# A decode layer on one core: weight rows in blocks of four, a bias added later, and stream buffers on 4 KB boundaries

## The chip, the cores and the metric

The kernel runs on one core of a Trainium2 chip. The metric is device time in microseconds (us) of one execution. Most executions of one kernel agree within 0.3%, which is 2 us here. Each kernel of the experiments was timed in rounds beside the kernel before, on the same chip.

## The reference

One decode step of a transformer layer in bf16: attention over a long cache, then an MLP with the mish activation.

```python
# B=4 sequences, one token each, D=640, H=32 heads, Sk=4096 cached keys, Dh=128, F=1728
q = (layernorm(x) @ wq)                              # wq [640, 4096]
p = softmax(q @ k_cache^T * Dh**-0.5)                # k_cache, v_cache [4, 32, 4096, 128]
h = x + (p @ v_cache) @ wo                           # wo [4096, 640]
g = layernorm(h) @ w1 + b1                           # w1 [640, 1728], b1 [1728]
act = g * tanh(log1p(exp(-|g|)) + max(g, 0))         # mish
out = h + act @ w2                                   # w2 [1728, 640]
```

The two caches are 268 MB of the 283 MB that the kernel reads.

## The kernel before

In what follows PE is the matmul engine, DVE the vector engine and ACT the activation engine; SP only issues loads and stores. A load has "landed" on a DMA engine when that engine has reported its share of it as done.

Everything large goes through four stream slots of 32 KB a partition. A cache tile is 4 MB: 128 partitions of one 32768 B row each. There are 64 such loads (the last is cut into four), and the weights travel in the same queue: wq first, wo between the tiles and at the end, then w1 into a slot, then w2 into a buffer of its own.

The sizes that matter: `P` = 128; `FM` = 13 full blocks of 128 MLP columns; `FT` = 64 columns left over, the "tail"; `DC` = 5 blocks of 128 in D; `FC` = 14; `N` = 4.

```python
consts = ctx.enter_context(tc.tile_pool(name="consts", bufs=1))
stream = ctx.enter_context(tc.tile_pool(name="stream", bufs=NSLOT))   # 4 slots, behind consts
...
w2_sb = consts.tile([P, FM, D], BF16)
W1S = (0, 2, 4, DC)
W2S = (0, 5, 10, FM)

def load_mlp():
    w1_slot = stream.tile([P, SLOT], BF16, tag="s", name="w1_slot")
    ...
    for c0, c1 in zip(W1S, W1S[1:]):                    # w1: three loads of 2, 2, 1 row blocks
        nc.sync.dma_start(out=w1_sb[:, c0:c1, :], in_=w1_v[:, c0:c1, :])
    w2_v = B_w2[0 : FM * P, :].rearrange("(p j) n -> p j n", j=FM)   # 13 rows per partition
    for j0, j1 in zip(W2S, W2S[1:]):                    # w2: three loads, 5, 5, 3 rows a partition
        nc.sync.dma_start(out=w2_sb[:, j0:j1, :], in_=w2_v[:, j0:j1, :])
...
# at the start: b1 turned onto partitions by the load itself, 26 B (and 2 B) a partition
nc.scalar.dma_start(out=b1T[:, 0:FM], in_=B_b1[0 : FM * P].rearrange("(p j) -> p j", j=FM))
nc.scalar.dma_start(out=b1T[0:FT, FM : FM + 1], in_=B_b1[FM * P : F].rearrange("(p o) -> p o", o=1))
...
        if i == 0:                                      # after the first cache tile
            nc.scalar.dma_start(out=w2_tail[0:FT, :], in_=B_w2[FM * P : F, :])
            nc.scalar.dma_start(out=w2_tail[FT : FT + CG, :], in_=B_w2[F - CG : F, :])
...
# MLP, at the end. b1 goes into the sum over w1, so it is multiplied by std first
b1s = b1T * std                                         # (cut to its meaning)
for c0, c1 in zip(W1S, W1S[1:]):
    if c1 == DC:
        nc.tensor.matmul(h1_ps[:, :, :], lhsT=ident_f[:, :], rhs=b1s[:, :, :], start=False, stop=False)
    for j in [FM] + list(range(FM)):
        for c in range(c0, c1):
            if j < FM:                                  # every 13th column of w1
                w = w1_sb[:, c, 0 : FM * P].rearrange("p (f j) -> p j f", j=FM)[:, j, :]
            else:
                w = w1_sb[:, c, FM * P : F]
            nc.tensor.matmul(h1_ps[0 : (P if j < FM else FT), j, :], lhsT=w, rhs=cen[:, c, :], ...)
h1 = h1_ps * rstd                                       # (cut to its meaning)
# ... mish: one activation and five vector operations, giving act
for j in [FM] + list(range(FM)):                        # 56 output matmuls
    for k in range(CG):
        nc.tensor.matmul(y2_ps[...], lhsT=act[0:rows, j, :],
                         rhs=w2_sb[:, j, cs] if j < FM else w2_tail[0:FT, cs], ...)
nc.vector.tensor_copy(out=o_bf[:, :], in_=y2_ps[:, :])  # then the store
```

A partition holds 13 consecutive rows of w2 so that each load has long rows. The price is that block `j` of the hidden vector is every 13th column of w1.

The softmax here doesn't subtract the row's maximum and nothing guards it: scores larger than these inputs give would overflow.

## Time and profile before

| | before |
|---|---|
| time, median of the first 3 runs | 669.73 us (669.3 to 670.16) |
| time, median of 6 runs, at the comparison | 669.35 us (668.91 to 670.16) |
| span of the profiled execution | 667.5 us |
| busy: PE, DVE | 426.0 us (64%), 411.7 us (62%) |
| bytes moved by DMA, mean rate | 283.81 MB, 425 GB/s |
| 32768 B packets (8192), median, mean | 1213, 1217.0 ns |
| 5120 B, 3456 B, 1280 B packets, median | 196, 135, 55 ns |

These lines are from the page of the kernel before. The span is cut into 40 slices. "DMA" is the mean busy share of the 16 DMA engines in tenths (9 means 90% or more), the next line the rate in each slice. The q lines give packets, megabytes and share of the engines' time: q1 is the SP queue with the stream, q10 the ACT queue with the small loads, and q8 instruction fetches.

```profile
DMA  9999999999999999999999999999999999999995
GB/s 376 440 411 438 419 438 435 432 427 439 432 427 430 430 436 429 438 437 423 432 437 431 433 428 436 437 430 427 434 437 436 429 429 432 438 431 430 427 415 241
DMA packets 12591, 283.81 MB, mean 425 GB/s; under 512 B 1608, under 2 KB 1680, under 8 KB 3728
q1 hardware_dynamic: 12224, 283.27, 98.8%
q8 instruction: 23, 0.38, 0.2%
q10 hardware_dynamic: 336, 0.10, 0.1%
```

The DMA engines are full in every slice but the last. The stream sets the time up to about 650 us. Only the last 15 us or so offer another choice. This is the end of the chain of waits that finished last (start, duration, what):

```profile
641.55 15.31 DMA w_slot<-in_B_w_dram
656.86 0.04 issue
656.90 1.89 PE h_ps L537 x28
658.80 0.52 PE h_ps L528 x2
659.32 1.02 PE h_ps L537 x14
...
661.91 0.23 DVE act L576
662.14 0.04 issue
662.18 2.16 PE y_ps L585 x55
664.34 0.02 issue
664.37 0.33 DVE o_bf L591
```

The second w1 load has landed at 656.86. Its 28 matmuls, the b1 matmul, the 14 matmuls of the third load, mish and the output matmuls follow without a gap. The last w2 load does not appear. Its landing is in the trace all the same: 658.38 us on the DMA engine that finished first, 662.96 on the one that finished last. A load is there only when the slowest of 16 engines is done.

Two groups of the timeline (start, duration, engine, line, operation, count) show why the choice of columns costs time:

```profile
649.25 0.67 PE L409 MATMUL y_ps<-a_2706,wo_late 128*128 128x4 bf16 x20
654.79 1.91 PE L537 MATMUL h_ps<-cen,w_slot 128*64 128x4 bf16 x28
```

Matmuls of one output size take 33 ns with wo's contiguous columns (0.67 us over 20) and 68 ns with every 13th column of w1 (1.91 over 28).

### The profile page before, as it was taken

To read this page: it belongs to the slowest core of one execution; us is meant where nothing else is said; L and a number is where in the kernel's file an instruction comes from. 1 tells how busy PE (TensorE), PEld (TensorE's weight loads), DVE (VectorE), ACT (ScalarE), POOL (GpSimd) and SP (SyncE) were. 2 spreads that over 40 slices of the span, in tenths; PEclk is the share of its full clock that TensorE was granted. 3 is DMA by queue.
4 is the path that set the end of the run, shared out by engine and by line. 5 is a ranking of instruction groups with operands and counts; after the bars stand their busy time and mean duration, and the time that the engine had idled before them with its cause. 6 is when DMAs were issued, how large, how long until landed. Compare 5 with 4: busy or idle time off the path is not lost.

```text
span 667.5 us, 6967 instructions
## 1 busy us (share of the span) xinstructions
PE 426.0 (64%) x2937; PEld 198.2 (30%) x2937; DVE 411.7 (62%) x477; ACT 75.5 (11%) x312; POOL 1.9 (0%) x9
## 2 busy tenths in 40 slices
PE   1967546694567675574764865568765657747586
PEld 0323222242223332232332422233322223323145
DVE  3387565686565676465675666557765657757542
ACT  0401001010001110011100110101100111001011
POOL 1000000000000000000000000000000000000000
PEclk9987789897788976788877788979867898778895
DMA  9999999999999999999999999999999999999995
GB/s 376 440 411 438 419 438 435 432 427 439 432 427 430 430 436 429 438 437 423 432 437 431 433 428 436 437 430 427 434 437 436 429 429 432 438 431 430 427 415 241
DMA packets 12591, 283.81 MB, mean 425 GB/s; under 512 B 1608, under 2 KB 1680, under 8 KB 3728
## 3 DMA queue, kind: packets, MB, share of 16 engines
q1 hardware_dynamic: 12224, 283.27, 98.8%
q8 instruction: 23, 0.38, 0.2%
q10 hardware_dynamic: 336, 0.10, 0.1%
q14 instruction: 8, 0.07, 0.0%
HBM read 283.36 MB, written 0.01 MB: 424 GB/s over the span
## 4 chain that ended last, share of the span: by engine, by line
DMA 61%; DVE 19%; PE 18%; issue 1%; ACT 0%; SPq 0%; DVEq 0%; ACTq 0%
DVE prod L284 16%; PE red L296 14%; DMA k_1005<-in_A_k_cache_dram 4%; DMA k_530<-in_A_k_cache_dram 4%; DMA k_1480<-in_A_k_cache_dram 4%; DMA k_1955<-in_A_k_cache_dram 4%; DMA k_2881<-in_A_k_cache_dram 4%; DMA k_2428<-in_A_k_cache_dram 4%; DMA k_3334<-in_A_k_cache_dram 4%; DMA k_1691<-in_A_k_cache_dram 4%; DMA k_310<-in_A_k_cache_dram 4%; DMA k_3092<-in_A_k_cache_dram 4%; DMA k_1216<-in_A_k_cache_dram 3%; DMA k_741<-in_A_k_cache_dram 3%; DMA v_3666<-in_A_v_cache_dram 3%; DMA k_2166<-in_A_k_cache_dram 3%
## 5 line engine op out<-in xcount | busy, mean ns | idle before, releaser
L296 PE MATMUL red<-prod,ident 128*128 128x512 bf16 x1024 | 300.1, 451 | 218.9 <-DVE prod L284 218.0
L296 PEld LDWEIGHTS <-ident 128*128 128x128 bf16 x1024 | 116.0, 114 | 385.2 <-issue 317.6
L313 DVE TENSOR_REDUCE s_f<-red 128x32 f32<-128x512 f32 x128 | 88.1, 688 | 79.4 <-PE red L296 79.2
L316 ACT ACTIVATE ex<-s_f 128x32 bf16<-128x32 f32 x128 | 29.3, 229 | 516.6 <-DVE s_f L313 516.6
L323 DVE TENSOR_TENSOR e<-ex,hmask 128x128 bf16<-128x128 bf16 x128 | 36.5, 285 | 6.1 <-ACT ex L316 6.1
L373 PEld LDWEIGHTS o_ps<-selo,pv_sb 128*128 128x128 f32 x256 | 34.0, 194 | 6.0 <-ACT pv_sb L363 1.2
L352 PEld LDWEIGHTS <-e 128*16 128x16 bf16 x1024 | 22.6, 89 | 36.8 <-issue 15.5
L373 PE MATMUL o_ps<-selo,pv_sb 128*128 128x4 f32 x256 | 31.1, 245 | 0.7 <-ACT pv_sb L363 0.7
L316 ACT ACTIVATION_READ_ACCUMULATOR ex<-s_f 128x1 f32 x128 | 23.9, 187 | 0.1
L284 DVE TENSOR_TENSOR prod<-k_79,qbc 128x4096 bf16<-128x4096 bf16 x4 | 9.1, 2287 | 17.6 <-DMA k_79<-in_A_k_cache_dram 17.6
L379 DVE TENSOR_TENSOR OT<-o_ps,rl 128x16 bf16<-128x16 f32 x8 | 1.6, 195 | 21.0 <-PE o_ps L373 21.0
L256 PE MATMUL q_ps<-wq_74,lnT 128*4 128x512 bf16 x32 | 10.7, 470 | 4.7 <-DMA wq_74<-in_A_wq_dram 4.7
L284 DVE TENSOR_TENSOR prod<-k_1691,qbc 128x4096 bf16<-128x4096 bf16 x4 | 9.1, 2286 | 5.7 <-DMA k_1691<-in_A_k_cache_dram 5.7
L284 DVE TENSOR_TENSOR prod<-k_3092,qbc 128x4096 bf16<-128x4096 bf16 x4 | 9.1, 2286 | 5.7 <-DMA k_3092<-in_A_k_cache_dram 5.7
L284 DVE TENSOR_TENSOR prod<-k_1216,qbc 128x4096 bf16<-128x4096 bf16 x4 | 9.1, 2286 | 4.9 <-DMA k_1216<-in_A_k_cache_dram 4.9
L284 DVE TENSOR_TENSOR prod<-k_3545,qbc 128x4096 bf16<-128x4096 bf16 x4 | 9.1, 2286 | 4.9 <-DMA k_3545<-in_A_k_cache_dram 4.9
L284 DVE TENSOR_TENSOR prod<-k_741,qbc 128x4096 bf16<-128x4096 bf16 x4 | 9.1, 2285 | 4.9 <-DMA k_741<-in_A_k_cache_dram 4.9
L284 DVE TENSOR_TENSOR prod<-k_903,qbc 128x4096 bf16<-128x4096 bf16 x4 | 9.1, 2287 | 4.8 <-DMA k_903<-in_A_k_cache_dram 4.8
L284 DVE TENSOR_TENSOR prod<-k_428,qbc 128x4096 bf16<-128x4096 bf16 x4 | 9.1, 2286 | 4.6 <-DMA k_428<-in_A_k_cache_dram 4.6
L284 DVE TENSOR_TENSOR prod<-k_1378,qbc 128x4096 bf16<-128x4096 bf16 x4 | 9.1, 2286 | 4.5 <-DMA k_1378<-in_A_k_cache_dram 4.5
L284 DVE TENSOR_TENSOR prod<-k_1853,qbc 128x4096 bf16<-128x4096 bf16 x4 | 9.1, 2286 | 4.5 <-DMA k_1853<-in_A_k_cache_dram 4.5
L284 DVE TENSOR_TENSOR prod<-k_530,qbc 128x4096 bf16<-128x4096 bf16 x4 | 9.1, 2285 | 4.4 <-DMA k_530<-in_A_k_cache_dram 4.4
(179 smaller groups left out, 376.2 us busy)
## 6 DMA issues: line engine op xcount, KB each, us to landing
wq_74<-in_A_wq_dram SPq DMA_DIRECT2D x1, 4096.0 KB
k_79<-in_A_k_cache_dram SPq DMA_DIRECT2D x1, 4096.0 KB, 24.8
k_81<-in_A_k_cache_dram SPq DMA_DIRECT2D x1, 4096.0 KB, 33.9
v_83<-in_A_v_cache_dram SPq DMA_DIRECT2D x1, 4096.0 KB, 17.3
k_244<-in_A_k_cache_dram SPq DMA_DIRECT2D x1, 4096.0 KB
v_246<-in_A_v_cache_dram SPq DMA_DIRECT2D x1, 4096.0 KB
k_310<-in_A_k_cache_dram SPq DMA_DIRECT2D x1, 4096.0 KB, 24.6
v_314<-in_A_v_cache_dram SPq DMA_DIRECT2D x1, 4096.0 KB, 32.1
```

The lines of the kernel that those rows point to most:

```text
L256: nc.tensor.matmul(q_ps[:, :], lhsT=lnT[:, c, :], rhs=wq_t[c // WQC][:, o : o + 512], start=(c == 0), stop=(c == DC - 1),)
L284: nc.vector.tensor_tensor(out=t[:, :, :], in0=kt[i][:, s * RS : (s + 1) * RS, :], in1=q_bc[hg][:, b, :].unsqueeze(1).to_broadcast([P, RS, ...
L296: nc.tensor.matmul(red[:, :, :], lhsT=ident[:, :], rhs=t[:, :, c * CW : (c + 1) * CW], start=(c == 0), stop=(c == Dh // CW - 1),)
L313: nc.vector.tensor_reduce(out=s_t[i][:, sl], in_=reds.pop((i, s))[:, :, :], axis=AX.X, op=ALU.add)
L316: nc.scalar.activation(out=ex_t[i][:, sl], in_=s_t[i][:, sl], func=ACT.Exp, scale=SCALE, accum_out=rs_t[hg][:, b, s : s + 1],)
L323: nc.vector.tensor_tensor(out=e_t[i][:, sl, :], in0=ex_t[i][:, sl].unsqueeze(2).to_broadcast([P, RS, G]), in1=hmask[:, :].unsqueeze(1).to_ ...
L352: nc.tensor.matmul(pvs[i % 2][k * QD : k * QD + RQ * G, :], lhsT=e_t[i][:, u * RQ : (u + 1) * RQ, :], rhs=vt[i][:, u * RQ : (u + 1) * RQ, ...
L373: nc.tensor.matmul(o_ps[hg][:, b, :], lhsT=t[:, r, :], rhs=selo[:, r, :], start=(r == 0), stop=(r == RQ - 1),)
L379: nc.vector.tensor_tensor(out=OT[:, hg * G : (hg + 1) * G, :].rearrange("p g b -> p b g"), in0=o_ps.pop(hg)[:, :, :], in1=rl.pop(hg)[:, :] ...
```

## The change

It has three intents. The slots shall start on 4 KB boundaries: 20480 B into the partition instead of 57600 B, which is 256 B past one. The MLP's rows are taken in blocks of four per partition, so that w1 is read at every 4th column instead of every 13th. And b1 is added behind rstd by one vector addition, so that its scaling and its matmul go. The loads change with it: w2 comes in four loads (three of 4 rows, one of 1 row a partition), its 64-row tail moves from the ACT queue near the start to the SP queue right before them, and b1 moves from the start to behind tile 1 and is cut into smaller pieces.

```diff
+    front = ctx.enter_context(tc.tile_pool(name="front", bufs=1))
+    stream = ctx.enter_context(tc.tile_pool(name="stream", bufs=NSLOT))
     consts = ctx.enter_context(tc.tile_pool(name="consts", bufs=1))
-    stream = ctx.enter_context(tc.tile_pool(name="stream", bufs=NSLOT))
...
-    W2S = (0, 5, 10, FM)
+    JW = 4
+    def fcols(t, j):
+        if j == FM:
+            return t[:, FM * P : F]
+        j0 = j - j % JW
+        w = min(JW, FM - j0)
+        return t[:, j0 * P : (j0 + w) * P].rearrange("k (p r) -> k r p", r=w)[:, j - j0, :]
...
-        w2_v = B_w2[0 : FM * P, :].rearrange("(p j) n -> p j n", j=FM)
-        for j0, j1 in zip(W2S, W2S[1:]):
-            nc.sync.dma_start(out=w2_sb[:, j0:j1, :], in_=w2_v[:, j0:j1, :])
+        nc.sync.dma_start(out=w2_tail[0:FT, :], in_=B_w2[FM * P : F, :])
+        for j in range(0, FM, JW):
+            w = min(JW, FM - j)
+            nc.sync.dma_start(
+                out=w2_sb[:, j : j + w, :],
+                in_=B_w2[j * P : (j + w) * P, :].rearrange("(p r) n -> p r n", r=w),
+            )
...
-    (the two b1 loads at the start)
+    def load_b1():
+        n = FM - FM % JW
+        nc.scalar.dma_start(
+            out=b1T[:, 0:n].rearrange("p (g r) -> p g r", r=JW),
+            in_=B_b1[0 : n * P].rearrange("(g p r) -> p g r", p=P, r=JW),
+        )
+        nc.scalar.dma_start(
+            out=b1T[:, n:FM], in_=B_b1[n * P : FM * P].rearrange("(p r) -> p r", p=P)
+        )
+        nc.scalar.dma_start(
+            out=b1T[0:FT, FM : FM + 1], in_=B_b1[FM * P : F].rearrange("(p o) -> p o", o=1)
+        )
+    front.tile([P, P], BF16, name="spacer")
     (ident, ones_f, zeros, ones_d, identw and w2_tail move to front; ident_f goes)
...
-        if i == 0:
-            (the two w2_tail loads)
+        if i == 1:
+            load_b1()
...
-    b1s = b1T * std2
-        if c1 == DC:
-            nc.tensor.matmul(h1_ps[:, :, :], lhsT=ident_f[:, :], rhs=b1s[:, :, :], ...)
...
     (h1 = h1_ps * rstd)
+    nc.vector.tensor_tensor(
+        out=h1[:, :, :], in0=h1[:, :, :],
+        in1=b1T[:, :].unsqueeze(2).to_broadcast([P, FC, N]), op=ALU.add,
+    )
```

More of the change, by code (lines that the diff above doesn't have):

```diff
@@ L74 @@
     b1_rem = consts.tile([1, P], BF16)
-    w2_tail = consts.tile([P, D], BF16)
+    w2_tail = front.tile([P, D], BF16)
     WQC = SLOT // (H * Dh)
@@ L154 @@
     nc.gpsimd.memset(b1T[:, :], 0.0)
-    nc.scalar.dma_start(out=b1T[:, 0:FM], in_=B_b1[0 : FM * P].rearrange("(p j) -> p j", j=FM))
-    nc.scalar.dma_start(
-        out=b1T[0:FT, FM : FM + 1], in_=B_b1[FM * P : F].rearrange("(p o) -> p o", o=1)
-    )
-    ident = consts.tile([P, P], BF16)
+    def load_b1():
[11 more added lines that the diff above has]
+    front.tile([P, P], BF16, name="spacer")
+    ident = front.tile([P, P], BF16)
     make_identity(nc, ident[:, :])
-    ones_f = consts.tile([P, P], FP32)
+    ones_f = front.tile([P, P], FP32)
     nc.vector.memset(ones_f[:, :], 1.0)
-    ident_f = consts.tile([P, P], FP32)
-    nc.vector.tensor_copy(out=ident_f[:, :], in_=ident[:, :])
     eps4 = consts.tile([P, 1], FP32)
     nc.vector.memset(eps4[:, :], EPS)
-    zeros = consts.tile([P, P], BF16)
+    zeros = front.tile([P, P], BF16)
     nc.vector.memset(zeros[:, :], 0.0)
@@ L203 @@
     nc.vector.tensor_copy(out=hmask[:, :], in_=hmask_f[:, :])
-    ones_d = consts.tile([P, P], FP32)
+    ones_d = front.tile([P, P], FP32)
     nc.vector.memset(ones_d[:, :], 1.0 / D)
     IW = D // CG
-    identw = consts.tile([P, 2 * IW + P], BF16)
+    identw = front.tile([P, 2 * IW + P], BF16)
     nc.gpsimd.memset(identw[:, :], 0.0)
@@ L441 @@
         emit_mask(i, NSUB - 1)
-        if i == 0:
-            nc.scalar.dma_start(out=w2_tail[0:FT, :], in_=B_w2[FM * P : F, :])
-            nc.scalar.dma_start(
-                out=w2_tail[FT : FT + CG, :], in_=B_w2[F - CG : F, :]
-            )
+        if i == 1:
+            load_b1()
         if i > 0:
@@ L509 @@
     )
-    b1s = consts.tile([P, FC, N], FP32)
-    nc.vector.tensor_tensor(
-        out=b1s[:, :, :], in0=b1T[:, :].unsqueeze(2).to_broadcast([P, FC, N]),
-        in1=std2[:, :].unsqueeze(1).to_broadcast([P, FC, N]), op=ALU.mult,
-    )
     rstd = consts.tile([P, N], FP32)
@@ L526 @@
     for c0, c1 in zip(W1S, W1S[1:]):
-        if c1 == DC:
-            nc.tensor.matmul(
-                h1_ps[:, :, :], lhsT=ident_f[:, :], rhs=b1s[:, :, :], start=False, stop=False
-            )
         for j in [FM] + list(range(FM)):
             for c in range(c0, c1):
-                if j < FM:
-                    w = w1_sb[:, c, 0 : FM * P].rearrange("p (f j) -> p j f", j=FM)[:, j, :]
-                else:
-                    w = w1_sb[:, c, FM * P : F]
                 nc.tensor.matmul(
-                    h1_ps[0 : (P if j < FM else FT), j, :], lhsT=w, rhs=cen[:, c, :],
+                    h1_ps[0 : (P if j < FM else FT), j, :],
+                    lhsT=fcols(w1_sb[:, c, :], j), rhs=cen[:, c, :],
                     start=False, stop=(c == DC - 1 and j == FM - 1),
```

## The prediction

> **What bounds the kernel now.** The loads. The table of 40 slices shows the DMA engines at 9 (90% or more) in 39 slices, 425 GB/s on average; PE is busy 64%, DVE 62%. In the trace's packet records the 8192 packets of 32768 B take 1213 ns each at the median, 1217 at the mean: 623 of the 661 us that all packets take per engine. From 1280 to 32768 B a packet takes about 8 ns + size/27.2 GB/s (1280: 55, 3456: 135, 5120: 196, 8192: 309 ns). That is already the ceiling that the Trainium skill, "SBUF — State Buffer", section "Door 1", gives (about 27.2 GB/s a port); only the 8 ns a packet are left, about 4.5 us in all.
>
> The chain of waits ends: second w1 chunk landing 656.86, 28 matmuls 1.89, b1 matmul 0.52, third chunk's 14 matmuls 1.02, mish chain 1.8 (act at 662.14), 55 output matmuls 2.16, copy 0.33, store to 667.5. The landings show w2 last at 662.96 on the slowest engine (658.4 on the fastest), just off the chain.
>
> **The change, costed.**
> 1. Slots from 256 past a 4 KB boundary onto one: I expect nothing. The case has its own test: of the five w1 rows of 3456 B in a slot the first crosses no 4 KB line, the others one each; all 640 packets took 135 ns. The 5120 B rows of wo took 196 ns in tiles 128 B off a 256 B line and in a slot on one. At most the 8 ns could go (512 packets an engine: 4.1 us).
> 2. w1 columns picked every 4 instead of every 13 elements. Weight loads set the pace here: 68 ns a matmul in the w1 groups (28 in 1.91 us), 33 in the wo groups with contiguous columns (20 in 0.67). The Trainium skill, "SBUF — State Buffer" (Specifications), asks for two hits a 16-byte line; every 4th bf16 gives two, every 13th one. I expect 33 to 45 ns: second chunk done about 657.9 instead of 658.8, third (landing 657.9) about 658.5.
> 3. b1 matmul (0.52 us, on the chain) and b1s (0.22, off it) go; one DVE add of 0.22 us comes onto it. Act ready about 660.5 instead of 662.1.
> 4. w2: the tail (80 KB) moves from the middle to the end of the stream, four blocks instead of three. After w1, per engine: 4x55 + 24x196 + 8x55 ns = 5.4 us instead of 5.1; the same 0.25 us leaves the middle. b1 becomes about 36 tiny packets an engine (9 ns each) instead of 12. Net about zero.
>
> **On the critical path.** The 1.7 us that PE and DVE gain does not all count, since w2's landing takes over: block 8 to 11 lands about 662.8, the last near 663.2, and only four matmuls are left; output sum about 663.6 instead of 664.34. Gain about 0.7 us (0.3 if the w1 loads don't speed up).
>
> **Prediction:** 668.9 us, range 666.8 to 669.9. Faster by over 2%: 0.01; within 2%: 0.98; slower: 0.01.
>
> **What will show it.** The w1 matmuls 33 to 45 ns apart; a DVE add near 0.22 us; act over 1 us earlier; output matmuls waiting for a w2 landing, which the chain then names; 32768 B packets still 1213 ns.
>
> **What would make it wrong.** If those packets fall towards 1205 ns, alignment is worth up to 4 us and the time goes to 665. If the stream's mean rate rises without the packets' median, the cause is contention I can't see here. If the unevenness of the engines (4.6 us between first and last) changes, the time moves by a microsecond either way. If the strided loads stay at 68 ns, the gain halves.

## The result, and the profile after

| | before | after |
|---|---|---|
| median of 6 runs each | 669.35 us (668.91 to 670.16) | 669.44 us (669.11 to 669.64) |
| span of the profiled execution | 667.5 us | 667.5 us |
| w1 landings, slowest engine | 654.75, 656.86, 657.90 | 655.05, 657.34, 658.53 |
| last w2 landing, slowest engine | 662.96 | 663.74 |
| act ready | 662.14 | 661.36 |
| last output matmul done | 664.34 | 664.26 |
| 32768 B packets, median, mean | 1213, 1217.0 ns | 1213, 1216.6 ns |

The ratio of after to before is 1.000, with a 95% interval of 0.9987 to 1.0013: the same. Here and below, a ratio is the mean time of one kernel's fast runs over that of the other's of the same rounds, so it is not quite the ratio of the medians quoted. The interval of ±0.9 us does not resolve the predicted gain of 0.8 us from none; the profiles and the experiments have to. All outputs are right.

The same lines of the page, after:

```profile
DMA  9999999999999999999999999999999999999996
GB/s 375 440 430 428 431 412 433 428 425 443 428 427 436 426 435 434 438 433 423 438 435 429 431 432 436 435 424 433 436 435 434 425 435 436 436 426 432 429 415 250
DMA packets 13128, 283.81 MB, mean 425 GB/s; under 512 B 2021, under 2 KB 2217, under 8 KB 4265
q1 hardware_dynamic: 12448, 283.35, 98.8%
q8 instruction: 23, 0.38, 0.2%
q10 hardware_dynamic: 648, 0.01, 0.1%
```

The bytes and the mean rate are the same, but q10 carries 648 packets instead of 336, for a tenth of the bytes. The lowest of the early slices has moved too. Before, it is the third (411 GB/s, 33 to 50 us), where the tail of w2 is loaded. After, it is the sixth (412 GB/s, 83 to 100 us), where the last of b1's pieces pass. By this count, which puts a packet into the slice in which it starts, a slow slice was not removed but moved.

The end of the chain of waits, after:

```profile
651.26 12.10 DMA w_sb<-in_B_w_dram
663.35 0.04 issue
663.39 0.86 PE y_ps L597 x15
664.26 0.02 issue
664.28 0.33 DVE o_bf L603
```

And the groups of the timeline that answer to the parts of the change:

```profile
655.09 1.20 PE L544 MATMUL h_ps<-cen,w_slot 128*64 128x4 bf16 x28 [0.23 <-DMA w_slot<-in_B_w_dram]
659.60 0.22 DVE L575 TENSOR_TENSOR h_4148<-h_4148,b1T 128x56 f32<-128x56 f32 x1
661.14 0.22 DVE L588 SCALAR_TENSOR_TENSOR act<-tb,hm_4147 128x56 bf16<-128x56 f32 x1
661.64 1.24 PE L597 MATMUL y_ps<-w_sb,act 128*4 128x160 bf16 x32
663.39 0.84 PE L597 MATMUL y_ps<-w_sb,act 128*4 128x160 bf16 x20 [0.51 <-DMA w_sb<-in_B_w_dram]
664.28 0.33 DVE L603 CAST o_bf<-y_ps 128x160 bf16<-128x160 f32 x1 [2.92 <-PE y_ps L597]
```

The compute part worked: 43 ns a matmul instead of 68 (1.20 us over 28), the b1 matmul is gone, and the addition costs 0.22 us. Act is ready 0.78 us earlier although w1 landed 0.3 to 0.6 us later. But the chain now goes past all that, through w2: after 32 output matmuls PE stands idle for 0.51 us until the third w2 block has landed at 663.35. It landed 0.39 us later than the whole of w2 had landed before. So the question is why the loads came later when their bytes are the same.

### The profile page after: what moved, and what is told of

The parts are those of the page before. It is cut to its first block, busy times and chain, and to the rows that moved or that the text cites. A ratio compares the mean times of both kernels' runs of the same rounds, so it can differ in the third digit from the quotient of the medians.

```text
span 667.5 us, 6964 instructions
## 1 busy us (share of the span) xinstructions
PE 423.1 (63%) x2935; PEld 195.5 (29%) x2935; DVE 411.1 (62%) x476; ACT 75.7 (11%) x312; POOL 1.9 (0%) x9
## 4 chain that ended last, share of the span: by engine, by line
DMA 64%; DVE 18%; PE 17%; issue 1%; ACT 0%; SPq 0%; DVEq 0%
DVE prod L307 16%; PE red L319 13%; DMA k_1956<-in_A_k_cache_dram 4%; DMA k_1481<-in_A_k_cache_dram 4%; DMA k_1006<-in_A_k_cache_dram 4%; DMA k_2429<-in_A_k_cache_dram 4%; DMA k_3335<-in_A_k_cache_dram 4%; DMA k_531<-in_A_k_cache_dram 4%; DMA k_2882<-in_A_k_cache_dram 4%; DMA wo_late<-in_A_wo_dram 4%; DMA k_1692<-in_A_k_cache_dram 4%; DMA k_3093<-in_A_k_cache_dram 4%; DMA k_2640<-in_A_k_cache_dram 3%; DMA k_3546<-in_A_k_cache_dram 3%; DMA k_1217<-in_A_k_cache_dram 3%; DMA k_308<-in_A_k_cache_dram 3%
```

## The experiments

The theory: the change adds two costs to the stream that the packet records hardly show, b1's small pieces and a tail that uses half of the partitions at the end; alignment is worth nothing at this size of step. The rivals: the new slot addresses matter in one direction or the other, the compute part bought nothing of itself, or the unevenness of the DMA engines just fell differently. Unless said otherwise, each kernel is the changed one with the edit shown. "Landed" means on the slowest engine. The kernels ran in three groups on three chips (e1 to e4, e5 to e8, e9 to e12), and the medians of the kernel before differ by 0.3 us between these groups (669.32 to 669.64), so a difference of some tenths between kernels of different groups is not resolved by the medians alone.

### Where the slots start: 256, 32 and 64 B past a 4 KB boundary

```diff
-    front.tile([P, P], BF16, name="spacer")
+    front.tile([P, 2 * P], BF16, name="spacer")      # e1_off256: slots at 20736
+    front.tile([P, P + 16], BF16, name="spacer")     # e2_off32:  slots at 20512
+    front.tile([P, P + 32], BF16, name="spacer")     # e9_off64:  slots at 20544
```

> The changed kernel with the spacer twice as wide, so that the four slots again start 256 B past a 4 KB boundary. Theory (alignment is worth nothing; the expected gain was eaten by small scattered loads): 32768 B packets 1213 ns at the median, last w2 landing within 0.2 us of the changed kernel's 663.7, time within 0.5 us of it. Rival (alignment helps by 1 us or more and something else cancels it): packets longer than 1213 ns or landings 1 us later, time 670.5 or more.

> The changed kernel with the slots 32 B past a 4 KB boundary, so not on a 256 B line either. Theory: still 1213 ns a packet and the same time within 0.5 us. Rival (the start of a slot matters once it leaves a 256 B line): packets about 8 ns longer, which over 512 packets an engine is 4 us: time about 673.5.

> The changed kernel with the slots 64 B past a 4 KB boundary. The slots at +32 B cost 3.1 us (packets of 32768 B 1216 instead of 1213 ns), those at +256 B nothing. Theory A (only a start off a 64 B line costs): 1213 ns, time within 0.5 us of 669.4. Rival B (any start off a 128 B line or more costs the same): 1216 ns and time near 672.5.

| slots start | median, us | before in the same rounds | ratio to before (95%) | 32768 B packets, median, mean |
|---|---|---|---|---|
| +256 | 669.42 | 669.64 | 0.9999 (0.9987 to 1.0012) | 1213, 1216.5 ns |
| +32 | 672.51 | 669.64 | 1.0046 (1.0032 to 1.0060) | 1216, 1221.0 ns |
| +64 | 672.16 | 669.44 | 1.0040 (1.0027 to 1.0052) | 1215, 1220.2 ns |

Off by 256 B, the position that the kernel before had, nothing changes: the first intent bought nothing because nothing was lost. Off by 32 or 64 B the kernel is about 3 us slower. The prediction ("I expect nothing") holds for its own case, the step of 256 B. What failed is my theory for the finer steps, 1213 ns and no change at +32; the rivals held there, e2's with 3 ns a packet instead of 8, and B in e9. My evidence had come from rows at 128 B off a 256 B line that took the usual 196 ns. They were rows of wo beside an aligned stream; a stream that is itself 128 B off was not tried.

The mean of the 32768 B packets rises by 4.4 ns at +32. With 512 such packets on each engine that is 2.3 us of the 3.1 us above the +0 kernel; the rest is spread over smaller packets, which also lie off the line in these two kernels because everything behind the slots shifts with them. The Trainium skill, "DMA: Bandwidth & Descriptors", section "How a descriptor splits into AXI transactions", says that a transaction must start on a 256 B address and that a descriptor starting elsewhere pays extra beats. The trace agrees in kind: +256 is free, +32 and +64 are not. It is my reading, not shown, that this is the mechanism on the SBUF side, and two things speak against it. By that account +64 would cost more than +32, and it cost less. And in the changed kernel wo's tiles in the middle start 160 B past a 256 B line (in a build of it), yet 501 of their 512 packets took 196 ns.

### b1's load: contiguous, half contiguous, tripled

The first kernel loads b1 as four contiguous rows (three of 1024 B, one of 384 B) and turns them onto partitions with six small matmuls while the stream runs. The second does so only for the last 192 values, so it keeps the 384 pieces of 8 B and drops the 192 pieces of 2 B. The third loads b1 two more times into tiles that nobody reads.

```diff
# e3_b1rows
-    (load_b1 as three scattered loads)
+        nc.scalar.dma_start(out=b1_a[:, :], in_=B_b1[0:n].rearrange("(g c) -> g c", g=NG))
+        nc.scalar.dma_start(out=b1_b[:, :], in_=B_b1[n:F].rearrange("(o c) -> o c", o=1))
+    def turn_b1():   # at tile 5: matmuls against ident[0:3, 0:3] and ident[0:1, 0:1], copies to b1T
# e10_b1part
-    (the two loads of 2 B pieces)
+        nc.scalar.dma_start(out=b1_b[:, :], in_=B_b1[n * P : F].rearrange("(o c) -> o c", o=1))
+    def turn_b1():   # at tile 5: two matmuls, two copies
# e4_b1x3
+        if i in (3, 5):
+            load_b1(consts.tile([P, FM + 1], BF16, name=f"b1X{i}"))
```

> The changed kernel with b1 loaded as 4 contiguous packets and turned by PE, instead of 576 packets of 8 and 2 B. Theory (the landings of before and after show that the 36 tiny packets an engine cost about 1.2 us of every engine's stream): first landings from the fifth tile on 1.0 to 1.3 us earlier than in the changed kernel, last w2 landing near 662.5, time 668.2 to 668.6. Rival (tiny packets cost 9 ns each, as their records say, and the later landings are chance or come from w2's blocks): landings 0.3 us earlier at most, time 669.1 or more.

> The changed kernel with the 384 pieces of 8 B of b1 still scattered, but its 192 pieces of 2 B loaded as one packet and turned by PE. In the changed kernel's packets the stream dips (to about 390 GB/s between 80 and 85 us) while the 2 B packets run, not while the 8 B packets run. Theory A (the 2 B pieces are most of b1's cost): first landings from about 95 us on 0.8 to 1.0 us earlier than in the changed kernel, time 668.4 to 668.8. Rival B (every interruption costs alike, 24 of 36 remain): 0.3 to 0.4 us earlier, time 669.0 to 669.2.

> The changed kernel with the scattered b1 load issued three times, twice into tiles that nobody reads. Theory: each further load of 576 tiny packets delays all later landings by about 1.2 us, so 2.4 us in all: time about 671.8. Rival: 36 packets of 9 ns are 0.3 us each, 0.6 in all: time about 670.0.

| kernel | median, us | ratio to before (95%) | last w2 landing | against after |
|---|---|---|---|---|
| after | 669.44 | 1.0000 (0.9987 to 1.0013) | 663.74 | |
| e10_b1part | 668.58 | 0.9986 (0.9973 to 0.9998) | 663.26 | 0.48 us earlier |
| e3_b1rows | 668.35 | 0.9984 (0.9971 to 0.9996) | 662.79 | 0.95 us earlier |

The tiny pieces cost about 1 us. The cleaner measure is the fourth V tile's load, taken on the first engine to finish it, so that the engines which instruction fetches have delayed do not count (a later section shows that these delay single engines): 104.65 us after, 104.00 in e10, 103.64 in e3. Read from these three profiles, the 12 pieces of 2 B that each engine handles cost 0.65 us, between the two theories of e10, and the 24 of 8 B cost 0.36 us. How far this can be trusted, other kernels show. Three with b1's loads unchanged, the tail at the end and the slots on a 256 B line (e1, e7, e11) have this load at 104.24 to 104.84 us, and e6 and e12, with b1 in rows, at 103.56 and 103.49. So the sum is 0.6 to 1.4 us. The split is not resolved by one profile each, but when the wo load before the third V tile lands, with nearly nine tenths of the 8 B pieces past and no 2 B piece, after stands level with e3 (74.61 against 74.60 us), so there the loss came with the 2 B pieces or with the last of the others. In the records each of these packets takes 9 ns, 0.32 us for all 36: the cost is two to four times that. Where it shows is in the rate while the pieces pass (58 to 94 us). The columns of this view are the window, its length, the busy time of PE, PE's weight loads, DVE, ACT and POOL with counts, the granted clock, the DMA share and the GB/s. First after, then e10:

```profile
80.00:85.00 5.00, 5.00 (x24) 2.48 (x22) 4.07 (x5) 0.65 (x4) 0.00 (x0) 0.76 0.96 393
85.00:90.00 5.00, 4.10 (x38) 1.64 (x40) 3.63 (x6) 0.65 (x4) 0.00 (x0) 1.00 0.95 400
```

```profile
80.00:85.00 5.00, 4.75 (x23) 2.54 (x22) 3.73 (x5) 0.53 (x4) 0.00 (x0) 0.85 1.00 433
85.00:90.00 5.00, 3.88 (x34) 1.58 (x35) 3.82 (x5) 0.57 (x5) 0.00 (x0) 1.00 0.99 426
```

With the 2 B pieces the engines are idle by this view for 4 to 5% of the time, and the rate is 393 and 400 GB/s instead of 433 and 426. A packet counts in the window in which it starts, so single windows swing: in the kernel before, 70 to 75 us reads 0.94 and 396 without any piece of b1. So I summed exactly what part of the time from 76 to 94 us the records cover. After leaves 0.42 us an engine uncovered, nearly all of it at 82 to 87 us, where the third V tile's load ends (84.62 on the first engine) and the next begins. The same b1 loads leave 0.52 us in e7, 0.46 in e11, 0.16 in e4, 0.08 in e1 and next to none in e5; e3, e6 and e10 leave none. This is time that no packet is charged with, and it is not a fixed price of the pieces.

An obvious rival is that the stream's queue ran empty, because its issue had to wait for b1's loads. After does show such waits of the SP queue (what for: us in total, times, longest):

```profile
SPq L98 <- DMA b1T<-in_B_b_dram: 28.3, 3, 12.5
```

But from 50 to 110 us each large load was issued at least 10 us before the one ahead of it landed on the first engine, so the queue was not empty. The Trainium skill, "DMA: Bandwidth & Descriptors" (Specifications), gives 512 B as the smallest transfer at full rate, with a read-modify-write below it. These runs agree that tiny pieces cost more than their bytes: 0.6 to 1.4 us for 24 of 8 B and 12 of 2 B an engine.

The tripled load gave 674.65 us, ratio 1.0078 (1.0066 to 1.0091): more than either theory expected, and it cannot be read as a dose. The reason is in the waits of the SP queue (what for: us in total, times, longest) and in the windows:

```profile
SPq L98 <- DMA b1X<-in_B_b_dram: 54.8, 4, 26.9
```

```profile
130.00:140.00 10.00, 7.54 (x84) 3.56 (x83) 5.40 (x8) 0.68 (x5) 0.00 (x0) 0.65 0.64 243
```

The queue that issues the stream stood waiting for the extra b1 loads, once for 26.9 us, and the stream ran dry at 130 to 140 us (DMA share 0.64, 243 GB/s). In 10 us at the usual 430 GB/s, (430 − 243)/430 × 10 us = 4.3 us were lost, an estimate from those two rates. That leaves about 1 us of the 5.2 us over after for the two more loads themselves. The landings on the first engine place it. Against after, tiles land 0.36 us early at 94.62 us, where the pieces of the first extra load begin to pass, still 0.08 us early at 133.61 us with nine tenths of them past, 4.40 us late at 157.45 us behind the dry stretch, and 5.83 us late at 179.79 us, when the second extra load has passed. So the first extra load cost about 0.3 us and the second about 1.4 us: again not a fixed price. The experiment also shows something else: a slow small load can hold up a large stream that has no use for its data, if the large loads' issue comes to wait for it.

### The tail of w2: put back, or read as 128 rows

The first kernel puts the tail's load back to where it was, on the ACT queue after the first tile. The second is e3 with the tail read as the last 128 rows of w2, of which the last 64 are used: twice the bytes, on all partitions. The third is the second with the third w2 block in two loads.

```diff
# e5_tailmid
-        nc.sync.dma_start(out=w2_tail[0:FT, :], in_=B_w2[FM * P : F, :])
+        if i == 0:
+            nc.scalar.dma_start(out=w2_tail[0:FT, :], in_=B_w2[FM * P : F, :])
# e6_tail128, on e3_b1rows
-        nc.sync.dma_start(out=w2_tail[0:FT, :], in_=B_w2[FM * P : F, :])
+        nc.sync.dma_start(out=w2_tail[:, :], in_=B_w2[F - P : F, :])
     (h1, b1, act and the output matmuls of the tail on partitions 64 to 127)
# e12_split, on e6_tail128
-        for j in range(0, FM, JW):
+        for j, a, b in ((0, 0, 4), (4, 0, 4), (8, 0, 2), (8, 2, 4), (12, 0, 1)):
```

> The changed kernel with the 64 rows of w2_tail loaded in the middle again (on ACT's queue, after the first tile, as before the change), the rest unchanged. Theory (a load of 64 partitions costs each engine 0.5 to 0.8 us wherever it stands, two to three times its own packet time): from w1's first landing to w2's last on the slowest engine 8.2 to 8.4 us instead of 8.7, landings in the middle 0.5 to 0.8 us later, so nothing is won: time within 0.4 us of 669.4. Rival (it costs its 0.22 us of packets): both shifts are 0.2 to 0.3.

> The kernel with b1 in rows (668.35 us), and the tail of w2 read as 128 rows, of which the last 64 are used: twice the bytes, but over all partitions. Theory (the 64-partition load is slow [...] and it holds up the engines that are still at w1): 3456 B packets back at 135 ns in the mean instead of 137, from w1's first to w2's last landing on the slowest engine 8.5 us or less instead of 8.8, time 0.2 to 0.4 us below 668.35. Rival (only bytes and packets count): 4 more packets of 55 ns an engine, 0.2 us slower than 668.35.

> The kernel with b1 in rows and w2's tail over 128 partitions (667.84 us), with the third block of w2 in two loads of two rows per partition, so that fewer matmuls are left after the last wait. Theory: 8 more packets an engine, 0.06 us; after the last wait 4 to 12 matmuls instead of 20, the output sum complete 0.1 to 0.4 us earlier: time 667.4 to 667.8. Rival: what the split wins the extra packets and landings lose, no change.

"End stage" is the time from the first w1 landing to the last w2 landing, both on the slowest engine.

| kernel | median, us | ratio to before (95%) | end stage | 3456 B packets, mean | last w2 landing |
|---|---|---|---|---|---|
| before | | 1 | 8.21 us | 135.0 ns | 662.96 |
| after | 669.44 | 1.0000 (0.9987 to 1.0013) | 8.69 us | 137.2 ns | 663.74 |
| e5_tailmid | 668.89 | 0.9994 (0.9981 to 1.0008) | 8.16 us | 135.0 ns | 663.35 |
| e3_b1rows | 668.35 | 0.9984 (0.9971 to 0.9996) | 8.79 us | 137.3 ns | 662.79 |
| e6_tail128 | 667.84 | 0.9978 (0.9966 to 0.9991) | 8.61 us | 135.8 ns | 662.59 |
| e12_split | 667.87 | 0.9975 (0.9963 to 0.9988) | 8.70 us | 135.8 ns | 662.40 |

With the tail at the end the stage is 0.5 us longer, twice the 0.22 us that its four packets an engine take by the records: its neighbours slow down too. All w1 packets took exactly 135 ns before and in e5, and up to 198 ns after. Summed an engine, w1's and w2's packets take 0.35 us more after than at their usual 135, 196 and 55 ns, 0.04 us more in e5, and 0.26 to 0.62 us more in the seven other kernels with the 64-row tail at the end and the slots on a 256 B line. In the medians e5 is 0.55 us under after, in line with the stage, though the intervals of the two ratios overlap. That it is the 64 partitions and not the bytes shows in e6, which moves twice the bytes and still lands 0.2 us sooner than e3; its median is 0.5 us lower, again with intervals of the ratios that overlap, on another chip. The packets show it more clearly: 137.3 ns in e3 against 135.8 in e6 for those of 3456 B, 199.6 against 196.3 for those of 5120 B, and the sum above falls from 0.44 us an engine in e3 to 0.03 in e6 and e12. The Trainium skill, "SBUF — State Buffer", section "Door 1", says that partitions 0 to 63 reach only 8 of the 16 ports. These runs agree that a load on half of the partitions costs more than its packets. That the packets for the tail meet others at those ports is my reading, not shown: no record names a port.

e6 is the best version found, 0.22% under the kernel before, and its interval (0.9966 to 0.9991) leaves out a ratio of 1. Its chain still ends with the wait for w2:

```profile
650.30 11.88 DMA w_sb<-in_B_w_dram
662.17 0.04 issue
662.22 0.86 PE y_ps L621 x20
663.08 0.03 issue
663.11 0.33 DVE o_bf L627
```

Splitting the third block leaves 12 matmuls behind its last landing instead of 20. In its profile the output sum came at 662.77 instead of 663.08, but the time did not fall (667.87 against 667.84, in different rounds). No difference is resolved.

One thing here remains open. Moving the tail away from the middle should have brought the stream forward there. Between e5 and after, the load of the second V tile does land 0.77 us later with the tail in the middle (64.00 against 63.23 us on the first engine), but by the fourth V tile the two are level (104.63 and 104.65). b1's pieces, which pass in between, cost 0.3 us in e5 and 0.6 to 1.3 us in the others, counted from the second V tile against e3. In e5 the idle time at 82 to 87 us is nearly missing, but why, and so why the two costs don't add up, I don't know.

### The compute part: b1 back on PE, and rows of 13 again

The first kernel brings b1s, ident_f and the fp32 matmul back and drops the vector addition. The second brings back the 13 rows a partition for w1, w2 and b1 (b1's pieces become 26 B) and keeps everything else, w2 in four loads too.

```diff
# e7_b1pe
+    b1s = b1T * std2
+        if c1 == DC:
+            nc.tensor.matmul(h1_ps[:, :, :], lhsT=ident_f[:, :], rhs=b1s[:, :, :], start=False, stop=False)
-    (h1 = h1 + b1T)
# e8_rows13
-        return t[:, j0 * P : (j0 + w) * P].rearrange("k (p r) -> k r p", r=w)[:, j - j0, :]
+        return t[:, 0 : FM * P].rearrange("k (p r) -> k r p", r=FM)[:, j, :]
-                in_=B_w2[j * P : (j + w) * P, :].rearrange("(p r) n -> p r n", r=w),
+                in_=B_w2[0 : FM * P, :].rearrange("(p r) n -> p r n", r=FM)[:, j : j + w, :],
-    (b1 in three loads of 8 B and 2 B pieces)
+    (b1 in two loads: 128 pieces of 26 B, 64 of 2 B)
```

> The changed kernel with b1 added as before the change: b1 times std on DVE, put into the sum by a PE matmul of 0.52 us, no DVE add. Theory (PE and DVE's gain is off the critical path, since the output sum waits for w2): act ready 0.2 to 0.4 us later than 661.4, the wait for w2 shrinks from 0.5 us to 0.1 to 0.3, output sum still complete near 664.3, time within 0.15 us of the changed kernel's. Rival (the chain through PE still ends last): output sum and time 0.3 us later.

> The changed kernel with the row blocks undone: 13 rows of w2 per partition, w1 columns every 13, so b1 is 128 packets of 26 B and 64 of 2 B instead of 576; w2 still in four loads of 5120, 5120, 5120 and 1280 B rows, b1 still behind rstd. Theory: w1 matmuls back at 68 ns, but all landings after the b1 load 0.7 to 0.9 us earlier, so the output sum is complete 0.4 to 0.9 us earlier than 664.26: time 668.5 to 669.0, FASTER than the changed kernel in spite of slower weight loads. Rival (the row blocks are what helps, by 1.7 us on PE): time 0.5 us or more above the changed kernel's.

| kernel | median, us | ratio to before (95%) | w1 done landing | act ready | last w2 landing |
|---|---|---|---|---|---|
| after | 669.44 | 1.0000 (0.9987 to 1.0013) | 658.53 | 661.36 | 663.74 |
| e7_b1pe | 669.43 | 1.0001 (0.9988 to 1.0013) | 659.04 | 661.86 | 664.21 |
| e8_rows13 | 669.00 | 0.9993 (0.9981 to 1.0006) | 658.00 | 661.74 | 663.24 |

Taking the b1 matmul back costs nothing. Its timeline shows why:

```profile
658.73 0.65 PE L550 MATMUL h_ps<-b1s,ident_f 128*128 128x56 f32 x2
659.32 0.73 PE L555 MATMUL h_ps<-cen,w_slot 128*64 128x4 bf16 x14
663.87 0.84 PE L604 MATMUL y_ps<-w_sb,act 128*4 128x160 bf16 x20 [0.49 <-DMA w_sb<-in_B_w_dram]
```

The b1 matmul fills time in which PE waits for the third w1 load (659.04) anyway, because the 28 matmuls before it are now short. From that landing to act it takes 2.82 us (after: 2.83), since the vector addition is saved, and PE still waits 0.49 us for w2 (after: 0.51), more than the 0.1 to 0.3 us expected: act came 0.5 us later, but so did all landings in this run. Once w1's columns are quicker, moving b1 behind rstd buys nothing.

The second kernel is the plainest verdict on the change. It undoes the part that sped PE up most and is not slower; if anything it is 0.4 us quicker than the changed kernel, though the intervals overlap. This is the timeline group of its last w1 matmuls and the output matmuls of its chain:

```profile
656.75 2.92 PE L537 MATMUL h_ps<-cen,w_slot 128*64 128x4 bf16 x42 [0.40 <-DMA w_slot<-in_B_w_dram]
```

```profile
661.78 2.16 PE y_ps L590 x56
```

PE takes about 69 ns a matmul again (2.92 us over 42), and its chain again runs through PE without waiting for w2. But the 26 B pieces are 12 packets an engine, with the tail's, instead of 36, and everything lands 0.5 us earlier. The gain on PE and the loss on b1's load are of the same size. They come as a pair as long as b1 is scattered by its load, because blocks of four are what cuts it into 8 B pieces; e3 keeps the one without the other. The column choice itself agrees in part with the Trainium skill, "SBUF — State Buffer" (Specifications), which asks for two hits per 16-byte line: 68 ns at a step of 13 bf16 elements, 43 ns at a step of 4. But contiguous columns took 33 ns, so two hits were not yet full speed here, as far as wo's matmuls can be compared with w1's.

### The spread of the engines: more instructions

The 4.6 us between the first and the last engine grow through the run, from about 1 us. In the packet records nearly every step falls together with one of the 23 instruction fetches of 16384 B (about 935 ns each): one engine is about 1.4 us further behind from then on. The records do not name the engines, so this is read from the order of the landings. This kernel adds 16 useless small matmuls to each tile, so that more instructions have to be fetched.

```diff
+        idle = ps.tile([P, N], FP32, tag="misc", name="idle")
+        for _ in range(16):
+            nc.tensor.matmul(idle[:, :], lhsT=zeros[:, :], rhs=zeros[:, 0:N], start=True, stop=True)
```

> The changed kernel with 512 more tiny PE matmuls that nobody reads (16 a tile, 0.6 us of idle PE time in each 20 us). Theory (a 16 KB instruction fetch holds one of the 16 engines up by about 1.4 us, and that is where the engines' 4.6 us of spread at the end comes from): 1024 more instructions are 4 more packets of 16384 B (27 instead of 23), the mean over the engines of the last landing rises by about 0.35 us, the slowest engine's by 0 to 1.5, time 0 to 1.5 us above 669.4. Rival (fetches are hidden, the spread has another cause): no change of mean or spread.

It ran 670.44 us, ratio 1.0016 (1.0002 to 1.0030), with four fetches more than the 23 shown above for before and after:

```profile
q8 instruction: 27, 0.44, 0.2%
```

The last w2 landing, averaged over the engines, is 0.30 us later than after (661.90 against 661.60), and on the slowest engine 1.2 us later (664.95 against 663.74). Four times 1.4 us over 16 engines would be 0.35 us on average. So fetches cost stream time, and what counts is whether they hit the engine that is already last. Before and after have 23 each, and their spread at the last V tile is 4.60 and 4.62 us, so this does not explain their difference. It is one reason why landings alone can scatter by some tenths from kernel to kernel.

## Why the prediction was right or wrong

- **The time.** 668.9 was predicted within 666.8 to 669.9, and "within 2%" at 0.98. Measured were 669.44, inside the range, and a ratio of 1.000. The gain of 0.8 us against 669.73 (0.7 us in the sum at the output matmuls) was not there. The range reached up to the time of the kernel before, so falling inside it says little, and the kernel before itself came out at 669.35 in the comparison.
- **Alignment worth nothing:** right, shown by the kernel at +256. Its evidence, rows across 4 KB lines and 128 B off a 256 B line, does not carry to finer steps, as +32 and +64 cost 3.1 and 2.7 us.
- **w1 matmuls at 33 to 45 ns:** right, 43 ns. **The vector addition near 0.22 us:** right.
- **Act about 660.5:** 661.36. The compute after the third w1 landing was as predicted within 0.3 us (2.83 us, predicted 660.5 − 657.9 = 2.6), but that landing came at 658.53 instead of 657.90.
- **w2's landing takes over the chain:** right, in the form predicted, with an idle stretch of 0.51 us before the output matmuls.
- **Block 8 to 11 landing about 662.8, the last near 663.2:** 663.35 and 663.74, each 0.5 us late. That is most of the 0.66 us by which the output sum was late (664.26 against 663.6).

The step that failed is the fourth, "Net about zero". It took the packet records for the cost of a load. Both of its terms were mis-sized. "36 tiny packets an engine (9 ns each)" is 0.32 us by the records and was 1.0 us in e3 against after (0.6 to 1.4 us over all kernels that can be compared). And "the same 0.25 us leaves the middle" balanced the tail's move. At the end the tail cost 0.5 us, because as a load on 64 partitions it slows w1's and w2's packets as well, as e5 and e6 show. In the middle nothing came back: b1's pieces took what the departure of the tail and of the old b1 load had freed, and at the fourth V tile the stream stood at 104.65 us after and at 104.50 before.

So the expected gain went two ways. The 1.7 us saved on PE were cut by the w2 landing, as predicted. What should have been left was then eaten by loads that land 0.5 us later than priced, through work that was added to the stream hundreds of microseconds earlier and to its end. What remained of it in the profile is 0.08 us (664.34 to 664.26). Mending both costs in e6 brought the last w2 landing to 662.59 and the time to 667.84, 1.6 us under after. Of that, 1.1 us came with b1's rows (e3), which its landings confirm (0.95 us); the other 0.5 us came with the tail on all partitions, of which the landings of the two profiles show 0.2.

## What to carry to other kernels

In a kernel whose loads run without a gap, a small load costs stream time wherever it is issued, and its packet records can understate it: compare when the same later tile lands with and without it, on the first engine to finish it. Load a small vector in contiguous rows and turn it on an engine that has time, rather than letting the load scatter it into 2 or 8 B pieces, and spread even a small remainder over all partitions. Before shortening compute at the end, see which landing comes next in line behind it; here the last of w2 was there on the slowest engine only 0.8 us after act was ready.

## What the Trainium skill lacked or had wrong

- "DMA: Bandwidth & Descriptors" says that transfers below 512 B are not at full rate, but gives no cost for tiny pieces scattered beside a running stream. Here 24 of 8 B and 12 of 2 B an engine cost the stream 0.6 to 1.4 us from kernel to kernel, while their records add up to 0.32 us.
- "DMA: Bandwidth & Descriptors" gives the beats of a misaligned start, but no time for a long descriptor. "SBUF — State Buffer", section "Operand start alignment", says that its runs timed nothing. Here slots starting 32 or 64 B off a 256 B line cost 3.1 or 2.7 us in 669 (packets of 32768 B: mean 1221.0 or 1220.2 ns instead of 1216.6), and 256 B off a 4 KB line cost nothing.
- "SBUF — State Buffer", section "Door 1", gives the slow rate of a load that reaches half of the ports; the page says elsewhere that DMA engines can contend there, but not what such a load costs its neighbours in a full stream. Here 64 rows of 1280 B made the stage 0.5 us longer instead of 0.22, w1's and w2's packets taking 0.26 to 0.62 us more an engine in eight kernels, and 0.03 us with twice the bytes on 128 partitions.
- "Runtime: NRT & Kernel Launch" (Instruction fetch mechanics) tells of the fetches in blocks of 16 KiB, but no page that I found gives what they cost the DMA engines of a full stream. Here 23 fetches of 16384 B each left one engine about 1.4 us behind; four more moved the last landing by 0.30 us on average and 1.2 us on the slowest engine.
